# One of four sets of a dense product by seven block products, and a batch of attention one piece later, in a fused attention and MLP kernel

## The chip, the cores and the metric

One Trainium2 chip, one core. The metric is device time in microseconds (us) for one execution, lower is better. Three engines do most of the work: TensorE multiplies matrices, VectorE and ScalarE take its results out of PSUM and work on them (PSUM is the memory that TensorE's products go to, SBUF the one where the program keeps its other tiles). GpSimd does smaller elementwise work, and SyncE issues the transfers. Most executions of one kernel agree within 0.3%; a few lie about 1% higher.

## The reference, cut to what matters

Attention with a decay per head, in blocks of 64 (batch 4, 8 heads, 768 positions, 64 numbers a head), gives x of 3072 x 512. Then comes a dense layer pair with gelu.

```python
for b in range(nb):                      # 12 blocks of 64
    intra = einsum('bhic,bhjc->bhij', qb, kb) * Dmask
    intra = einsum('bhij,bhjd->bhid', intra, vb)
    inter = einsum('bhid,bhde->bhie', qb * lam_pow, kv_state)
    out[:, :, sl] = intra + inter
    kv_state = lam_block * kv_state + einsum('bhsd,bhse->bhde', kb_dec, vb)
...
h = x @ w_in                             # 512 x 2048, the first dense product
return gelu_tanh(h) @ w_out              # 2048 x 512, the second
```

## The kernel before

Attention is cut into 24 steps (4 batches, 3 blocks of 256 positions, 2 halves of the heads). From step 13 on the steps run in pairs (17 alone), called batches here: `burst((18, 19), (16, 17))` computes the scores of 18 and 19, the outputs O of 16 and 17, and the state products K of 18 and 19. The dense work is cut into pieces in a queue, `filler`, and `fill(n)` runs the next n of them between the attention batches, so that TensorE has work while VectorE and ScalarE prepare. Dense work is queued by groups of 256 or 512 tokens; group 4 is the fifth.

```python
groups = [[0, 1], [2], [3], [4, 5], [6, 7], [8, 9], [10, 11]]
SEVEN = (5, 6)                           # groups whose first product uses seven block products
...
def mm1(fs):                             # a plain piece: 4 matmuls of 512 columns, then gelu
    Hps = ps_M.tile([P, per, N], FP32, tag="M", name="Hps")
    for i, f in enumerate(fs):
        for c in range(NC):
            pin(nc.tensor.matmul(by_block(Hps[:, i, :]), w_in16[:, c, f * P : (f + 1) * P], x(c), ...))
    ...
    pin(nc.scalar.activation(out=dst, in_=Hps[:], func=AF.Gelu_apprx_tanh))
...
def sum_x(m):                            # one of four sums of blocks of x, on VectorE, fp16
    pin(nc.vector.tensor_tensor(x_block(m, cs), x_block(a, cs), x_block(b, cs), op))
...
def seven(m, k):                         # product m of set k: 4 matmuls of 256 columns
    ...                                  # into a bank HX (m = 1, 6, 7, 4), HW (2) or HY (5, 3)
    if m == 1:
        copied("m1", "q32", nc.scalar)   # ScalarE copies PSUM into a buffer of the q32 ring
    elif m == 2:
        added(0, 0, "m1")                # VectorE: m1 += HW; its gelu is put on `pending`
    elif m == 5:
        copied("q", "q32", nc.scalar)
        release()                        # runs what is pending
    elif m == 6:
        copied("u2", "k32", nc.vector)
    elif m == 3:
        added(0, 1, "u2")
    elif m == 7:
        added(1, 1, "q")                 # VectorE: q += HX
    elif m == 4:
        pending.insert(0, lambda: gelu(1, 0, dst[:]))
    if k == HF // 2 - 1 and m in (3, 7, 4):
        release()
...
for i in range(HF):                      # groups that use plain pieces
    for fs in ([[i, i + HF]] if per == 2 else [[i], [i + HF]]):
        filler.append(lambda fs=fs: mm1(fs))
```

`prep_qk(n)` is two things: VectorE and ScalarE cast q and k of step n to fp16 (`cast_qk`), and SyncE issues the DMA that transposes them (`transpose_dma`). `prep_v(n)` has GpSimd scale v of step n (`scale_v`) and issues the loads of step n + 3. `causal` is VectorE's masking of the scores. In the part concerned, the order of the program is this:

```python
    cast_qk(16)
    scale_v(16)
    fill(2)
    burst((13, 14), (12,))
    transpose_dma(16)
    ...
    fill(3)
    burst((15, 16), (13, 14))
    ...
    sum_win(4, 1, nc.vector)
    fill(2)
    prep_qk(20)
    fill(1)
    prep_qk(21)
    prep_v(20)
    fill(3)

    burst((18, 19), (16, 17))
    prep_v(21)
    fill(2)
    U(18)
    U(19)
    fill(4)
    prep_qk(22)
    fill(2)
    burst((20, 21), (18, 19), 11, 4)
```

## Time and profile before

| | value |
|---|---|
| time before, three runs | 199.60, 199.63, 201.62 us |
| time of the profiled run | 201.31 us, of which the trace's span is 199.4 us |
| busy | TensorE 96%, VectorE 77%, ScalarE 62%, GpSimd 38% |

The lines themselves stand in the prediction. How to read the table: TensorE is the bound, so only its work and its holes count. The profiled run took 201.31 us (a trace's span is some 1.9 us shorter than the time of its run).

### The profile page before, as it was taken

What the parts mean: (1) busy time and instruction counts of PE and PEld (TensorE: products, weight loads), DVE (VectorE), ACT (ScalarE), POOL (GpSimd) and SP (SyncE); (2) the same over time, 40 slices, a digit from 0 to 9 for tenths busy, and PEclk for the clock granted to TensorE, in tenths of its full rate; (3) what the DMA queues carried; (4) which work ended last, traced back from release to release, by engine and by line L of the source; (5) the groups of instructions that cost most, each with busy time, mean ns of one, the idle gap of its engine ahead of it and who ended that gap; (6) DMA issues with size and microseconds to landing.
All of it is one profiled execution on the core that took longest, in us unless ns stands there. A gap on an engine that the chain in (4) does not pass through costs nothing.

```text
span 199.4 us, 5931 instructions
## 1 busy us (share of the span) xinstructions
PE 191.8 (96%) x2437; PEld 140.4 (70%) x2439; DVE 152.9 (77%) x296; ACT 122.7 (62%) x251; POOL 74.8 (37%) x85
## 2 busy tenths in 40 slices
PE   8979999999999999969999999999999999999993
PEld 2556544456888888634578855578888888888882
DVE  4897623689997889968899927999678997588620
ACT  2673878366793675657764386764668845778321
POOL 6694123457457833547171535347002030002000
PEclk9999999999999999999999999999999999999999
DMA  6999999999999999999993997620202200020205
GB/s 173 290 327 386 386 384 384 294 287 294 327 246 262 219 280 149 221 299 221 302 195 62 249 324 92 184 56 0 52 26 83 104 9 0 0 108 0 105 3 210
DMA packets 61722, 37.86 MB, mean 190 GB/s; under 512 B 17536, under 2 KB 54656, under 8 KB 61696
## 3 DMA queue, kind: packets, MB, share of 16 engines
q1 hardware_dynamic: 61152, 37.23, 73.7%
q8 instruction: 19, 0.31, 0.7%
q10 hardware_dynamic: 544, 0.26, 0.5%
q14 instruction: 7, 0.06, 0.1%
HBM read 27.26 MB, written 6.29 MB: 168 GB/s over the span
## 4 chain that ended last, share of the span: by engine, by line
PE 75%; DMA 15%; SPq 6%; ACT 1%; issue 1%; DVE 1%
PE Hps L542 18%; PE MX L619 17%; PE MY L619 9%; PE HX L711 7%; DMA wi<-in_moe_w_in_dram 7%; DMA k<-in_k_dram 5%; PE MW L619 4%; SPq L70 4%; PE HY L711 4%; PE S L340 3%; PE O2ps L557 3%; DMA qkT<-qk 3%; PE HW L711 2%; SPq L94 2%; PE OK L398 1%; PE O L449 1%
## 5 line engine op out<-in xcount | busy, mean ns | idle before, releaser
L542 PE MATMUL Hps<-xT,w_in 128*128 128x512 f16 (+1 forms) x288 | 50.8, 332 | 0.0
L501 POOL TENSOR_TENSOR u<-t,lumask 128x256 f16<-128x256 f32 x40 | 30.6, 780 | 48.0 <-DVE t L494 30.5
L542 PEld LDWEIGHTS <-w_in 128*128 128x128 f16 x288 | 27.8, 98 | 19.0
L546 ACT ACTIVATE gT<-Hps 128x512 f16<-128x512 f32 x56 | 33.1, 598 | 9.4 <-PE Hps L542 8.8
L350 DVE TENSOR_TENSOR PT<-S,mask 128x512 f16<-128x512 f32 x48 | 30.4, 681 | 7.9 <-PE S L340 7.8
L619 PEld LDWEIGHTS <-gs 128*128 128x128 f16 x320 | 31.2, 98 | 3.6
L266 POOL TENSOR_TENSOR v<-v,dv 128x512 f16<-128x512 f32 x24 | 29.8, 1243 | 8.9 <-DMA v<-in_v_dram 8.4
L619 PEld LDWEIGHTS <-gT 128*128 128x128 f16 x240 | 23.2, 98 | 3.6 <-ACT gT L546 0.5
L619 PE MATMUL MX<-w_sum,gs 128*128 128x256 f16 x160 | 21.4, 273 | 0.0
L664 POOL TENSOR_TENSOR o<-u,q 128x512 f32<-128x512 f32 (+1 forms) x5 | 5.8, 1160 | 37.1 <-ACT u L636 37.1
L278 DVE TENSOR_TENSOR qk<-q,dq 128x512 f16<-128x512 f32 x23 | 19.0, 828 | 0.7 <-DMA q<-in_q_dram 0.6
L283 ACT ACTIVATE qk<-k 128x512 f16<-128x512 f32 x24 | 15.0, 626 | 6.5 <-DMA k<-in_k_dram 6.5
L589 DVE TENSOR_TENSOR gs<-gT 128x1024 f16<-128x1024 f16 (+1 forms) x24 | 16.6, 695 | 2.2 <-ACT gT L546 2.2
L557 PE MATMUL O2ps<-w_out,gT 128*128 128x512 f16 x64 | 14.6, 379 | 0.0
L475 ACT ACTIVATE xT<-OK 128x256 f16<-128x256 f32 x26 | 10.0, 455 | 7.3 <-PE OK L398 7.2
L711 PEld LDWEIGHTS <-ws 128*128 128x128 f16 x128 | 12.5, 98 | 1.8
L636 ACT ACTIVATE u<-MX 128x256 f32<-128x256 f32 x18 | 6.9, 384 | 10.2 <-PE MX L619 10.2
L475 ACT ACTIVATE xT<-O 128x256 f16<-128x256 f32 x22 | 8.0, 459 | 7.5 <-PE O L449 5.0
L340 PEld LDWEIGHTS <-qkT 64*64 64x64 f16 x384 | 6.0, 106 | 8.4 <-issue 2.5
L340 PE MATMUL S<-qkT 64*64 64x128 f16 x384 | 9.2, 221 | 2.6 <-DMA qkT<-qk 1.5
L589 DVE TENSOR_TENSOR gs<-gs,gT 128x1024 f16<-128x1024 f16 (+1 forms) x12 | 10.6, 887 | 0.3
L557 PEld LDWEIGHTS <-gT 128*128 128x128 f16 x64 | 6.1, 98 | 6.6
(95 smaller groups left out, 320.9 us busy)
## 6 DMA issues: line engine op xcount, KB each, us to landing
q<-in_q_dram SPq DMA_DIRECT2D x24, 256.0 KB, 5.1
k<-in_k_dram SPq DMA_DIRECT2D x24, 256.0 KB, 5.1
v<-in_v_dram SPq DMA_DIRECT2D x23, 256.0 KB, 5.3
out_dram<-o SPq DMA_DIRECT2D x19, 256.0 KB, 3.7
wo<-in_moe_w_out_dram SPq DMA_DIRECT2D x4, 1024.0 KB, 9.5
wi<-in_moe_w_in_dram SPq DMA_DIRECT2D x4, 512.0 KB, 8.2
wi<-in_moe_w_in_dram SPq DMA_DIRECT2D x2, 1024.0 KB, 12.8
out_dram<-o SPq DMA_DIRECT2D x2, 512.0 KB, 6.9
```

What stands on the lines that cost most here:

```text
L266: pin(nc.gpsimd.tensor_tensor(wide(tv[:]), ld32[s][2][:], decay(dv, s), ALU.mult))
L278: pin(q_eng.tensor_tensor(wide(tq), q32[:], decay(dq, s), ALU.mult))
L340: pin(nc.tensor.matmul(Sps[hl][half64(c), hp, jk, :], o[half64(hl), 1, jk, hp, half64(c)], o[half64(hl), 0, :, hp, half64(c)], start=True, ...
L350: pin(nc.vector.tensor_tensor(t[:, hl].rearrange("p b c d -> p b (c d)"), Sps[:].rearrange("p b c d -> p b (c d)"), mask[:].unsqueeze(1).t ...
L475: pin(nc.scalar.activation(out=d, in_=o, func=AF.Copy))
L501: pin(nc.gpsimd.tensor_tensor(u[:], state[half][:].unsqueeze(2).to_broadcast([P, 2, 2, D]), lumask[:, 2 * half : 2 * half + 2, :].unsqueez ...
L542: pin(nc.tensor.matmul(by_block(Hps[:, i, :]), w_in16[:, c, f * P : (f + 1) * P], x(c), start=(c == 0), stop=(c == NC - 1)))
L546: pin(nc.scalar.activation(out=dst, in_=Hps[:], func=AF.Gelu_apprx_tanh))
L557: pin(nc.tensor.matmul(O2[tau][0][:], gT[:, f % HF, f // HF, tau * P : (tau + 1) * P], w_out16[:, f, :], start=(n == 0), stop=(n == NF - 1)))
L589: pin(nc.vector.tensor_tensor(g_rows(m, i), g_rows(a, i), g_rows(b, i), op))
L619: pin(nc.tensor.matmul(dst, lhsT, rhs, start=(opens and i == 0), stop=(closes and i == HF - 1), skip_group_check=True))
L711: pin(nc.tensor.matmul(dst[:, i, :], w_in_block(a, slice(c, c + 1), slice(f * P, f * P + P))[:, 0], x_block(b, slice(c, c + 1))[:, 0], sta ...
```

## The change

The intent has two parts. The first: a batch of steps 13 and 14 waited for the transpose of step 14, so it starts one piece later, and the load of v of step 16 moves behind that transpose. The second: one of the four sets of group 4's first product is done by seven products of 256 columns in place of four pieces of 4 x 512, which is an eighth less TensorE work for that set; the preparations of steps 20 and 21 and the batch of 18 and 19 move to fit.

```diff
     SEVEN = (5, 6)
+    MIXED = 4
+    sum_xs = []
...
-            if k == HF // 2 - 1 and m in (3, 7, 4):
+            if (k == HF // 2 - 1 or g == MIXED) and m in (3, 7, 4):
                 release()
...
-        for i in range(HF):
+        if g == MIXED:
+            sum_xs.append(sum_x)
+            plain = [[f] for i in range(2, HF) for f in (i, i + HF)]
+            for m in (1, 0, 2, 5, 0, 6, 3, 0, 7, 4):
+                filler.append((lambda m=m: seven(m, 0)) if m else (lambda fs=plain.pop(0): mm1(fs)))
+            for fs in plain:
+                filler.append(lambda fs=fs: mm1(fs))
+        for i in range(HF) if g != MIXED else ():
...
-        prep_qk(n + 2) if n == 8 else prep(n + 2)
+        prep_qk(n + 2)
+        if n == 11:
+            scale_v(13)
+            load_step(16, "qk")
+        elif n > 8:
+            if n == 12:
+                load_step(16, "v")
+            prep_v(n + 2)
...
-    fill(2)
+    fill(3)
     burst((13, 14), (12,))
...
-    fill(3)
+    fill(2)
     cast_qk(17)
...
-    fill(2)
+    for m in (1, 2, 3, 4):
+        sum_xs[0](m)
     prep_qk(20)
-    fill(1)
+    fill(3)
     prep_qk(21)
+    fill(8)
+
+    burst((18, 19), (16, 17))
     prep_v(20)
-    fill(3)
-
-    burst((18, 19), (16, 17))
-    prep_v(21)
     fill(2)
     U(18)
     U(19)
-    fill(4)
+    prep_v(21)
+    fill(2)
     prep_qk(22)
     fill(2)
     burst((20, 21), (18, 19), 11, 4)
```

(Cut: the numbering of the pieces behind which VectorE's sums for the second product hang, which follows the three pieces more.)

More of the change, by code (lines that the diff above doesn't have):

```diff
@@ L862, in queue_group @@
         else:
-            behind(9, 0, 4, (1, 2) if g == 3 else (1, 2, 4, 3))
+            n1 += 3 * (g == MIXED)
+            behind(n1 - 7, 0, 4, (1, 2) if g == 3 else (1, 2, 4, 3))
             if g == 3:
```

## The prediction

> **What bounds the kernel now.** I read the page first: how busy each engine is, and in which slices.
>
> ```profile
> PE 191.8 (96%) x2437; PEld 140.4 (70%) x2439; DVE 152.9 (77%) x296; ACT 122.7 (62%) x251; POOL 74.8 (37%) x85
> PE   8979999999999999969999999999999999999993
> PEclk9999999999999999999999999999999999999999
> ```
>
> TensorE (PE) is busy for 191.8 of 199.4 us at full clock, so a microsecond counts only if it takes TensorE work away or closes a hole in that row. The row has holes at both ends, which the change does not touch, and one inside: slice 18 of 40 (a slice is 5 us), near 85 to 90 us. Next I asked who waited for whom on TensorE; the longest line is the hole:
>
> ```profile
> PE S L340 <- DMA qkT<-qk: 1.5, 1, 1.5
> ```
>
> The timeline of all engines from 80 to 92 us shows what it is:
>
> ```profile
> 82.39 0.45 SPq L70 DMA_DIRECT2D v<-in_v_dram  x1
> ...
> 83.00 1.72 SPq L293 DMA_TRANSPOSE qkT<-qk  x1
> ...
> 87.05 0.42 PE L340 MATMUL S<-qkT 64*64 64x128 f16 x16
> ...
> 88.41 4.07 SPq L293 DMA_TRANSPOSE qkT<-qk  x2
> ...
> 88.99 0.42 PE L340 MATMUL S<-qkT 64*64 64x128 f16 x16 [1.52 <-DMA qkT<-qk]
> ...
> 89.96 2.32 PE L542 MATMUL Hps<-xT,w_in 128*128 128x512 f16 x10
> ```
>
> This is the batch of steps 13 and 14. Scores of 13 run at 87.05; scores of 14 wait 1.52 us for the transposed q and k of step 14, whose transpose entered the queue at 83.00 behind the loads of q, k and v of step 16. The two transposes at 88.41 are those of 15 and 16, which matter below. The chain of waits gives that transpose's landing:
>
> ```profile
> 83.00 5.94 DMA qkT<-qk
> ```
>
> So it landed at 88.94. From there to the end the chain is TensorE nearly throughout.
>
> **What the Trainium skill says.** "TensorE: Matmul & The Clock Gate", Back-to-back issue gap, gives 262 cycles for 256 columns and 518 for 512, that is 109 and 216 ns at 2.4 GHz. The trace agrees: 28 matmuls of 512 columns fill 6.04 us of the chain (216 ns each), and four of 256 take a slot of 0.44 us. "DMA: Bandwidth & Descriptors", Queues, rings and completion order, says that each DMA engine takes descriptors in ring order. The trace agrees in direction: the transpose behind three loads took 5.94 us, one issued at 107.10 with no DMA running took 3.2. "VectorE: DVE Perf Modes", perf-mode tier table, has tensor_tensor at single rate with a PSUM operand and at double rate with 16-bit SBUF operands; here 0.69 us for an add of 512 columns from PSUM, 0.41 us for an fp16 sum of 512 columns. It agrees.
>
> **The change, part by part.** (1) The batch of 13 and 14 starts one dense piece later (4 matmuls of 512, 0.87 us), and the load of v16 moves behind the transpose of 14. Scores of 13 then begin at 87.05 + 0.87 = 87.92, those of 14 want to begin at 88.2. The transpose is issued 0.6 us earlier (82.4) with one 256 KB load less ahead (estimate 0.9 us at about 290 GB/s), so it should land near 88.05. The wait of **1.52 us goes**, entirely or all but 0.1.
>
> (2) The next batch (15 and 16) then comes sooner, but its transposes do not. The issuing queue is serial: the transpose of 15 is at 88.41 after the same set of issues, that of 16 at about 90.3 behind it. Those near there took 5.0 to 5.2 us to land, so 16 lands near 95.3. TensorE gets there earlier than before: scores of 14 at 88.2, dense work from 89.17, six pieces (24 x 0.216 = 5.2) instead of seven, scores of 15 at 94.45, of 16 at 94.73. A **new wait of about 0.6 us** on the transpose of 16 (in the kernel before TensorE came at 96.4, after the landing).
>
> (3) One of four sets of group 4's first product: 4 pieces of 4 x 512 columns (16 x 0.218 = 3.49 us) become 7 products of 4 x 256 (7 x 0.438 = 3.07 us). **0.42 us less TensorE work.** VectorE gets four fp16 sums (some 1.5 us), three adds and a copy (4 x 0.69); ScalarE two copies more (0.60 each). Before, VectorE stood idle 3.60 us ahead of the causal masks of that batch and ScalarE also had gaps, and the batch itself moves some 1.3 us back, so as totals they fit.
>
> (4) But the products share one PSUM bank HX, and they are queued as 1, 2, 5, 6, 3, 7, 4 with plain pieces after 1, 5 and 3 and **none between 7 and 4**. The built program's list of waits confirms it: the first matmul of 4 waits for VectorE's add that reads HX after 7. Group 5 already does the same products, spaced. Its timeline gives the latency:
>
> ```profile
> 140.06 0.60 PE L711 MATMUL HX<-xs,ws 128*128 128x256 f16 x4
> 140.49 0.60 PE L619 MATMUL MX<-w_sum,gs 128*128 128x256 f16 x4
> 140.69 0.69 DVE L732 TENSOR_TENSOR q<-HX,q 128x512 f32<-128x512 f32 x1
> ```
>
> Product 7 starts at 140.06, VectorE's add runs from 140.69 to 141.38. TensorE's next piece started at 140.49, so an adjacent product 4 would have stood for 141.38 - 140.49 = 0.89 us plus a few hundredths for the signal: **0.93 us added**. The other waits inside the set (6 on ScalarE's copy of 1, 3 on its copy of 5, 7 on VectorE's copy of 6) have 0.15 to 0.4 us to spare by my placing of the pieces.
>
> (5) The batch of 18 and 19 now stands after more pieces, and between it and the batch of 20 and 21 six pieces are left instead of eight: 5.25 us instead of 7.0. What has to happen inside that gap is not shorter. The transposes of 20 and 21 reuse buffers that the batch of 18 and 19 still reads; in the kernel before they were issued back to back:
>
> ```profile
> 113.86 1.69 SPq L643 DMA_DIRECT2D out_dram<-o  x2
> 120.57 2.65 SPq L293 DMA_TRANSPOSE qkT<-qk  x2
> ```
>
> The new order of the queue puts the second 512 KB output store between the two (it moved behind the transpose of 20, which blocks it until the batch is done). With X the issue of transpose 20, 1.75 us after the batch's start, transpose 21 was issued at X + 1.4 and landed at X + 5.5; now it is issued at about X + 2.2 with 512 KB ahead of it (estimate 1.4 us of data), landing between X + 6 and X + 7. Scores of 21 used to be due at about X + 7.3, now at X + 5.5. Likewise GpSimd's scaling of v20 and v21 moved into the gap: before, GpSimd did two u, v21 and two u in 4.3 us; one more scaling of 1.2 us ends about 8.7 us after the batch's start, where the K product of 21 is due at about 8.2. The two waits lie on top of each other, so the longer counts: **0.7 us added**, from 0.4 to 1.7.
>
> Sum: -1.52 + 0.6 - 0.42 + 0.93 + 0.7 = **+0.3 us**, so 199.63 + 0.29 = 199.9 us. After the batch of 20 and 21 the two programs have the same work left and TensorE is the bound to the end, so a shift there reaches the end whole.
>
> **The rivals.** First, the plain one that the intent suggests: the hole closes, the set saves its columns, no new wait: 199.63 - 1.52 - 0.42 = 197.7 us. Against it speaks the wait of 4 on 7, which the build shows, and the fixed issue of transpose 16. For it, that the order of the preparations was moved with some care. Second, transposes 16 and 21 land in time (the lag from data to landing varies) and only the wait of 4 on 7 stays: -1.52 - 0.42 + 0.93 = -1.0, so 198.6 us. Third, transpose 21 lands last behind the store, at X + 7.2 or later, and the small waits inside the set bite as well: +1 us more than my sum, 200.9 us. Fourth, VectorE becomes the bound around 105 to 120 us, where it has no idle time before the 3.60 us: then the waits spread over the set and come to some 0.5 us more, inside the third.
>
> **Range and chances.** The ends are the second and the third: 198.6 to 200.9. A step of 2% is 4 us; the largest gain I can construct is 1.9 us and the largest loss some 2, so "within 2%" has nearly all the chance: 0.02 faster, 0.97 same, 0.01 slower. The sign is close to open, leaning a little to slower.
>
> **What would show it.** In the changed profile: the 1.5 us wait of the scores on a transpose near 88 us is gone; a wait of 0.3 to 0.9 us on a transpose stands at the scores of step 16 near 95 us; a TensorE hole of about 0.9 us ahead of the last HX product near 119 us, released by VectorE's q add; a wait for a transpose or for GpSimd's v at the batch near 127 to 129 us. The prediction is wrong if the hole ahead of the last product is missing, if transpose 16 moves earlier together with TensorE, or if transpose 21 lands before its scores are due: each makes it faster by 0.6 to 0.9 us.

## The result, and the profile after

The changed kernel took 202.32 us as the median of six runs (201.91 to 203.12); the kernel before beside it took 199.62 (199.53 to 201.62, six runs). Ratios here are the mean time of one kernel's fast runs over that of the other's of the same rounds, so they are not quite the ratio of these medians: 1.012, 95% interval 1.0078 to 1.0163. That is within the 2% that counts as the same, but slower, and above the range that the prediction gave.

The page of the changed kernel: TensorE is as busy as before, but the span is 201.3 us.

```profile
PE 192.3 (96%) x2451; PEld 141.5 (70%) x2451; DVE 159.8 (79%) x304; ACT 123.8 (61%) x253; POOL 74.7 (37%) x85
PE   8979999999999999998999989799999999999993
```

The hole of slice 18 is gone, and there are new ones in slices 19, 24 and 26: one between 90 and 96 us, two between 115 and 131 us. Busy time doesn't show the 0.42 us that the set saves; the profile only models the ends of matmuls, so I count from starts below. TensorE's waits in the changed kernel (total, times, longest):

```profile
PE S L340 <- DMA qkT<-qk: 1.9, 2, 1.1
...
PE HX L713 <- DVE q L734: 0.8, 1, 0.8
...
PE Hps L544 <- DVE PT L350: 0.5, 1, 0.5
```

The first of the experiments ran the kernel before again, unchanged. That profile is of a run of 199.67 us, its span is 197.8 us, and it is the one to compare with. TensorE's longest wait in it is one at the start of the kernel, and no wait for a transpose is left:

```profile
...
PE idle L181 <- PEq L1083: 0.8, 1, 0.8
```

TensorE's timeline of this usual run of the kernel before, from the batch of 13 and 14 to the first dense piece after the batch of 20 and 21 (start, duration, what; x32 is the scores of two steps in one row, x16 of one):

```profile
87.08 0.64 PE L340 MATMUL S<-qkT 64*64 64x128 f16 x32
...
103.99 0.42 PE L340 MATMUL S<-qkT 64*64 64x128 f16 x16
...
117.19 0.64 PE L340 MATMUL S<-qkT 64*64 64x128 f16 x32
...
125.92 0.64 PE L340 MATMUL S<-qkT 64*64 64x128 f16 x32
...
127.46 2.75 PE L542 MATMUL Hps<-xT,w_in 128*128 128x512 f16 x12
```

The same places in the changed kernel, with the wait ahead of a row in brackets:

```profile
87.89 0.64 PE L340 MATMUL S<-qkT 64*64 64x128 f16 x32
...
95.67 0.42 PE L340 MATMUL S<-qkT 64*64 64x128 f16 x16 [0.84 <-DMA qkT<-qk]
...
104.98 0.42 PE L340 MATMUL S<-qkT 64*64 64x128 f16 x16
...
118.54 0.60 PE L713 MATMUL HX<-xs,ws 128*128 128x256 f16 x4
119.92 0.60 PE L713 MATMUL HX<-xs,w_in 128*128 128x256 f16 x4 [0.78 <-DVE q L734]
120.45 0.64 PE L340 MATMUL S<-qkT 64*64 64x128 f16 x32
...
127.45 0.42 PE L340 MATMUL S<-qkT 64*64 64x128 f16 x16
...
128.93 0.42 PE L340 MATMUL S<-qkT 64*64 64x128 f16 x16 [1.06 <-DMA qkT<-qk]
...
131.00 2.75 PE L544 MATMUL Hps<-xT,w_in 128*128 128x512 f16 x12 [0.50 <-DVE PT L350]
```

From that last row to the end both take 70.3 us, so the whole difference is ahead of it. From the scores of step 17 (103.99 before, 104.98 after) to that row it is 23.47 us before and 26.02 after: 2.55 us more. In parts:

- To the scores of 18 it is 2.27 us more. Two plain pieces, 1.75 us, moved ahead of that batch, and the set saves 0.42; that makes 1.33 of it. The other **0.94 us** is the hole ahead of product 4. The starts say the same: product 4 starts 1.38 us behind product 7, where undisturbed products start 0.44 us apart.
- From there to the scores of 20 it is 1.73 us less, which is the two pieces that moved away.
- From there to the dense row it is 3.55 us instead of 1.54: **2.01 us** more. The scores of 21 start 1.48 us behind those of 20, in the rerun of the kernel before 0.25, so 1.23 is the transpose of 21. The other 0.78 is VectorE: the dense row waits for its masks.

### The profile page after: what moved, and what is told of

Read it like the earlier page. It is cut to its first block, busy times and chain, and to the rows that moved or that the text cites. A ratio compares the mean times of both kernels' runs of the same rounds, so it can differ in the third digit from the quotient of the medians.

```text
span 201.3 us, 5970 instructions
## 1 busy us (share of the span) xinstructions
PE 192.3 (96%) x2451; PEld 141.5 (70%) x2451; DVE 159.8 (79%) x304; ACT 123.8 (61%) x253; POOL 74.7 (37%) x85
## 4 chain that ended last, share of the span: by engine, by line
PE 81%; DMA 6%; DVE 5%; SPq 4%; issue 1%; ACT 1%
PE Hps L544 18%; PE MX L621 17%; PE MY L621 9%; PE HX L713 8%; PE O2ps L559 7%; PE MW L621 4%; PE HY L713 4%; SPq L70 4%; DMA wi<-in_moe_w_in_dram 4%; PE Hps L804 3%; PE S L340 3%; DMA qkT<-qk 3%; PE HW L713 2%; DVE gs L591 2%; DVE PT L350 2%; PE OK L398 2%
## 5 line engine op out<-in xcount | busy, mean ns | idle before, releaser
L544 PE MATMUL Hps<-xT,w_in 128*128 128x512 f16 (+1 forms) x272 | 47.7, 329 | 0.5 <-DVE PT L350 0.5
L544 PEld LDWEIGHTS <-w_in 128*128 128x128 f16 x272 | 26.2, 98 | 17.4 <-issue 0.6
L548 ACT ACTIVATE gT<-Hps 128x512 f16<-128x512 f32 x52 | 30.7, 602 | 8.7 <-PE Hps L544 8.2
L621 PEld LDWEIGHTS <-gT 128*128 128x128 f16 x240 | 23.2, 98 | 3.6 <-ACT gT L548 0.5
L591 DVE TENSOR_TENSOR gs<-gT 128x1024 f16<-128x1024 f16 (+1 forms) x24 | 19.1, 802 | 1.2 <-ACT gT L548 1.2
L278 DVE TENSOR_TENSOR qk<-q,dq 128x512 f16<-128x512 f32 x23 | 19.6, 853 | 0.6 <-DMA q<-in_q_dram 0.5
L713 PEld LDWEIGHTS <-ws 128*128 128x128 f16 x144 | 14.0, 97 | 2.4
L713 PEld LDWEIGHTS <-w_in 128*128 128x128 f16 x108 | 10.5, 98 | 2.6 <-issue 1.0
L713 PE MATMUL HX<-xs,ws 128*128 128x256 f16 x72 | 10.8, 273 | 0.0
```

What stands on the lines that cost most here:

```text
L278: pin(q_eng.tensor_tensor(wide(tq), q32[:], decay(dq, s), ALU.mult))
L591: pin(nc.vector.tensor_tensor(g_rows(m, i), g_rows(a, i), g_rows(b, i), op))
L621: pin(nc.tensor.matmul(dst, lhsT, rhs, start=(opens and i == 0), stop=(closes and i == HF - 1), skip_group_check=True))
L713: pin(nc.tensor.matmul(dst[:, i, :], w_in_block(a, slice(c, c + 1), slice(f * P, f * P + P))[:, 0], x_block(b, slice(c, c + 1))[:, 0], sta ...
```

## The experiments

Two theories went into the first round. V: the 1.52 us hole near 88 us belongs to the one profiled run of the kernel before and not to its usual run, so part 1 of the change gains nothing. L: part 1 does gain, and the set loses still more than the timeline says. Each kernel is given as an edit of the kernel before or of the changed one. Medians of different rounds are compared only by their distance from the kernel before of the same round, which was 199.6 to 199.9 us throughout.

**b_again**: the kernel before, no edit.

> The kernel before, unchanged, to get a second profile of it. Its first profile has a span of 199.4 us and comes from a run of 201.3 us, while its timed runs are mostly 199.6 us: the profile may show a run that is not the usual one. Theory H (the hole is usual): the span is 199.4 again or near it, and the wait of the scores of step 14 on its transpose is 1 us or more. Theory V (the hole varies): the span is about 197.8 us and the wait near 88 us is 0.3 us or less, so that closing it was worth nothing in the usual run and the whole of the loss is the four new waits. Time: ratio 1.000 within 0.005.

Measured: 199.99 us (199.59 to 200.72), ratio 1.0016 [0.9995, 1.0036]; the hole near 88 us isn't there (the timeline above). SyncE's queue shows why. The first two rows are from the first profile of the kernel before, the transposes of steps 12 and 13:

```profile
71.46 4.13 SPq L293 DMA_TRANSPOSE qkT<-qk  x1
...
78.09 3.01 SPq L293 DMA_TRANSPOSE qkT<-qk  x1
```

The same two in the rerun:

```profile
71.36 1.80 SPq L293 DMA_TRANSPOSE qkT<-qk  x1
...
75.65 1.70 SPq L293 DMA_TRANSPOSE qkT<-qk  x1
```

In the first profile these two issues took 4.13 and 3.01 us, in the rerun 1.80 and 1.70, and the queue reached the transpose of 14 at 83.00 instead of 81.27. Why an issue sometimes takes 4 us I can't say. That the other long runs of the kernel before (5 of 68 in all were above 201 us) have the same hole isn't shown either: no second one of them was profiled. The profiles of `set_only` and `b_qk22` below, which leave this part as it was, don't have it.

**a_only**: part 1 alone, on the kernel before.

```diff
-        prep_qk(n + 2) if n == 8 else prep(n + 2)
+        prep_qk(n + 2)
+        if n == 11:
+            scale_v(13)
+            load_step(16, "qk")
+        elif n > 8:
+            if n == 12:
+                load_step(16, "v")
+            prep_v(n + 2)
...
-    fill(2)
+    fill(3)
     burst((13, 14), (12,))
...
-    fill(3)
+    fill(2)
```

> The kernel before with only the first part of the change: the batch of 13 and 14 one piece later, the load of v16 behind the transpose of 14. Theory H: gains 1.5 us at the scores of 14, loses 0.7 to 0.9 at the scores of 16 (transpose of 16 lands near 95.4), so 0.6 us faster, 199.0 us. Theory V: no gain to be had; the time is equal within 0.3 us or up to 0.8 us slower if the wait for the transpose of 16 is new.

Measured: 199.84 us, ratio 1.0008 [0.999, 1.0026]. Part 1 is worth nothing in usual runs.

**set_only**: the changed kernel with part 1 undone.

```diff
-        prep_qk(n + 2)
-        if n == 11:
...
-            prep_v(n + 2)
+        prep_qk(n + 2) if n == 8 else prep(n + 2)
...
-    fill(3)
+    fill(2)
     burst((13, 14), (12,))
...
-    fill(2)
+    fill(3)
```

> The changed kernel with the first part undone: the set of seven products and the moved preparations stay, the batch of 13 and 14 and the load of v16 are as in the kernel before. By the two traces, from the start of the set on, the change loses 0.94 (product 4 behind 7), 1.2 (scores of 21) and 0.6 (VectorE's masks) and saves 0.42 of TensorE work: 2.3 us slower than the kernel before, 201.9 us. If the losses were due to the first part (TensorE arriving earlier at transposes that do not), it is less than 1.5 us slower.

Measured: 202.58 us (201.91 to 204.23), ratio 1.0161 [1.0124, 1.0199]. From the scores of 17 to the dense row it takes 26.01 us, like the changed kernel's 26.02, with the same three waits. So the whole loss is the set and the preparations that moved with it, and theory V stands.

**spaced**: one plain piece between products 7 and 4, taken from the gap ahead of the batch of 20 and 21.

```diff
-            for m in (1, 0, 2, 5, 0, 6, 3, 0, 7, 4):
+            for m in (1, 0, 2, 5, 0, 6, 3, 0, 7, 0, 4):
...
-    fill(8)
+    fill(9)
     burst((18, 19), (16, 17))
...
-    fill(2)
+    fill(1)
     U(18)
```

> The changed kernel with one plain piece between products 7 and 4 of the set (and so one piece fewer after the batch of 18 and 19). Theory: VectorE's add of 0.69 us hides behind a piece of 0.87 us, TensorE's hole of 0.78 us ahead of product 4 is gone, but the gap between the batches has 5 pieces instead of 6, so the wait at the scores of 21 is up to 0.87 us longer: time within 0.3 us of the changed kernel. Rival: the wait at the scores of 21 is bound to the issue of its transpose, which follows the batch of 18 and 19 wherever that stands, so removing the hole just moves it: the sum of the two waits stays at 1.8 to 2.1 us.

Measured: 202.11 us, ratio 1.0148 [1.0108, 1.0189], like the changed kernel. (Its profile fell on an unusually long run, so only its waits are used.) The hole ahead of 4 is gone, and the scores of 21 wait that much longer:

```profile
129.27 0.42 PE L340 MATMUL S<-qkT 64*64 64x128 f16 x16 [2.00 <-DMA qkT<-qk]
```

(That is 0.94 us more than the 1.06 of the changed kernel.)

The second round asked about the gap ahead of the batch of 20 and 21. SyncE's queue in the changed kernel has the transposes of 20 and 21 with an output store between them, as predicted:

```profile
122.20 2.00 SPq L293 DMA_TRANSPOSE qkT<-qk  x1
124.31 0.52 SPq L645 DMA_DIRECT2D out_dram<-o  x1
125.00 1.53 SPq L293 DMA_TRANSPOSE qkT<-qk  x1
```

VectorE's timeline in the changed kernel ends the gap with the cast of step 22's q and the masks of 20 and 21:

```profile
125.44 1.42 DVE L591 TENSOR_TENSOR gs<-gs,gT 128x1024 f16<-128x1024 f16 x1
...
128.81 1.53 DVE L278 TENSOR_TENSOR qk<-q,dq 128x512 f16<-128x512 f32 x1
130.26 2.47 DVE L350 TENSOR_TENSOR PT<-S,mask 128x512 f16<-128x512 f32 x4
```

The same in the rerun of the kernel before:

```profile
123.19 0.98 DVE L589 TENSOR_TENSOR gs<-gs,gT 128x1024 f16<-128x1024 f16 x1
...
125.72 0.68 DVE L278 TENSOR_TENSOR qk<-q,dq 128x512 f16<-128x512 f32 x1
126.39 2.48 DVE L350 TENSOR_TENSOR PT<-S,mask 128x512 f16<-128x512 f32 x4
```

**store_first**: the transpose of 20 one piece later, so that the store precedes it and the two transposes are issued together.

```diff
+    fill(1)
     prep_qk(20)
-    fill(3)
+    fill(2)
     prep_qk(21)
```

> The changed kernel with one thing mended: the second output store of the group before is issued ahead of the transpose of 20 again, not between the transposes of 20 and 21. Theory D (VectorE's queue is what limits the gap between the two batches): the wait of the scores of 21 on their transpose (1.06 us in the changed kernel) shrinks by 0.5 us or more, but the masks of 20 still begin when VectorE has done its work (130.3 us), so the wait for them grows by about as much and the time stays within 0.3 us of the changed kernel's 202.3. Theory T (the transpose limits): the time falls by the length of the wait, to 201.3 us or less.

Measured: 203.14 us, ratio 1.0146 [1.0101, 1.019]. The scores of 21 no longer wait, and nothing is won: the next wait was ready right behind the first. TensorE in this run:

```profile
129.67 0.32 PE L438 MATMUL K<-v,qk 64*64 64x64 f16 x16 [0.98 <-POOL v L266]
...
130.82 2.75 PE L544 MATMUL Hps<-xT,w_in 128*128 128x512 f16 x12 [0.50 <-DVE PT L350]
```

GpSimd's scaling of v21 and VectorE's masks end about when the transpose used to. The prediction had the first of these ("the two waits lie on top of each other"); the masks it had not.

**qk22_late**: step 22's casts and transpose behind the batch of 20 and 21.

```diff
-    prep_qk(22)
     fill(2)
     burst((20, 21), (18, 19), 11, 4)
+    prep_qk(22)
```

> The changed kernel with the preparation of q and k of step 22 (1.5 us on VectorE in that place) moved behind the batch of 20 and 21, so that VectorE reaches the masks of 20 sooner. The transposes stay as they are. Theory D: the wait of TensorE on the masks (0.50 us at 131.0) is gone, the wait of the scores of 21 (1.06 us) stays: 0.5 to 0.7 us faster than the changed kernel, 201.7 us. Theory T: the masks are late only because the scores are: no change.

Measured: 201.65 us, ratio 1.0085 [1.0038, 1.0132]. The wait for the masks is gone and the one for the transpose of 21 stays at 1.09 us. Against the kernel before of its round it loses 1.9 us by the medians, where the changed kernel lost 2.7 of its own. In the profiles, scores of 17 to dense row take 25.35 us instead of 26.02, 0.67 less: most of the masks' 0.78 us, so their share of the gap was real and had its own cause.

**b_qk22**: the control, the same edit on the kernel before.

> A control: the kernel before with q and k of step 22 prepared behind the batch of 20 and 21, as in the mended kernel. VectorE's masks kept TensorE nowhere in the kernel before, so the ratio should be 1.000 within 0.002; if it is faster, part of what the mended kernel gains is not the set's.

Measured: 199.93 us, ratio 1.0008 [0.9988, 1.0029]. The kernel before, whose cast took 0.68 us, has nothing to win there.

**gap9**: three pieces more ahead of the batch of 20 and 21.

```diff
     prep_qk(22)
-    fill(2)
+    fill(5)
     burst((20, 21), (18, 19), 11, 4)
```

> The changed kernel with nine plain pieces between the batches of 18, 19 and of 20, 21 instead of six (7.9 us for 5.2), the last three taken from behind. Both waits in the gap, on the transpose of 21 and on the masks, should be gone (1.06 and 0.50 us by the records, 1.9 us of start times), and only the hole ahead of product 4 stays: 0.5 us slower than the kernel before, 200.4 us. If the time stays above 201.5 us, what is lost in that stretch is not the shortness of the gap.

Measured: 208.13 us, ratio 1.0398 [1.0352, 1.0444]; a clear miss. The waits in the gap are gone (20 and 21 in one row at 130.81). But the batch also sets where the sevenfold sets of group 5 fall against the attention that follows, and there VectorE now comes late (also 1.38 us for the masks at 163.31):

```profile
143.15 0.60 PE L713 MATMUL HX<-xs,ws 128*128 128x256 f16 x4 [2.26 <-DVE u L726]
```

The recorded waits, with the 0.78 us ahead of product 4, come to 5.6 of the 8.4 us by which this profile is longer than that of `b_again`. That the place of the sets is the reason is read from these waits; no run tested it.

**repaired**: the order of `spaced`, the store first, and two pieces more in the gap.

```diff
-            for m in (1, 0, 2, 5, 0, 6, 3, 0, 7, 4):
+            for m in (1, 0, 2, 5, 0, 6, 3, 0, 7, 0, 4):
...
+    fill(1)
     prep_qk(20)
-    fill(3)
+    fill(2)
     prep_qk(21)
-    fill(8)
+    fill(9)
...
     prep_qk(22)
-    fill(2)
+    fill(4)
     burst((20, 21), (18, 19), 11, 4)
```

> The changed kernel with three things mended together: a plain piece between products 7 and 4, eight plain pieces in the gap between the batches, and the store ahead of the transposes. No TensorE wait of the change is left, and the 0.42 us of saved columns should show: 0.2 to 0.5 us faster than the kernel before, ratio 0.998. Rival: the set costs more than it saves even when spaced (more weight loads, VectorE and ScalarE fuller), and the ratio is 1.003 or more.

Measured: 205.44 us, ratio 1.0265 [1.0226, 1.0304]; a miss of the same kind as `gap9` (waits of 1.73 us for VectorE's u and 1.03 us for its masks in group 5's stretch).

The third round mended without moving the batches.

**order7**: the same seven products and the same three plain pieces, with the piece that stood behind product 1 moved between 7 and 4.

```diff
-            for m in (1, 0, 2, 5, 0, 6, 3, 0, 7, 4):
+            for m in (1, 2, 5, 0, 6, 3, 0, 7, 0, 4):
```

> The changed kernel with the same three plain pieces placed otherwise in the set: 1, 2, 5, piece, 6, 3, piece, 7, piece, 4, so that each product that waits for a copy or an add out of its bank has at least 0.87 us of other work ahead, and the gap between the batches keeps six pieces. If the 0.78 us hole ahead of product 4 was a cost of its own, the batch of 18 and 19 comes 0.9 us earlier and all that follows with it, the waits in the gap staying what they are: 0.8 to 1.0 us faster than the changed kernel, 201.4 us. If the waits in the gap are tied to something that does not move with the batch, they grow by as much and the time stays at 202.3.

Measured: 201.37 us (201.1 to 201.75), ratio 1.0082 [1.006, 1.0104]; 1.77 us above the kernel before, where the changed kernel is 2.70 above. The hole ahead of product 4 is its own cost, of about the size predicted: by the medians its removal gained 0.93 us, and in the profiles the way from the scores of 17 to the dense row is 25.29 us instead of 26.02, 0.73 less (the K products now wait 0.27 us for ScalarE's gelu).

**gap_mended**: the three edits for the gap together: store first, step 22 late, and v20 scaled ahead of the batch.

```diff
+    fill(1)
     prep_qk(20)
-    fill(3)
+    fill(2)
     prep_qk(21)
+    scale_v(20)
     fill(8)

     burst((18, 19), (16, 17))
-    prep_v(20)
+    load_ahead(23)
+    prep_v(21)
     fill(2)
     U(18)
     U(19)
-    prep_v(21)
     fill(2)
-    prep_qk(22)
     fill(2)
     burst((20, 21), (18, 19), 11, 4)
+    prep_qk(22)
```

> The changed kernel with all three limits of the gap taken away and the numbers of pieces kept: the store ahead of the transposes of 20 and 21, v20 scaled on GpSimd before the batch of 18 and 19, q and k of 22 prepared behind the batch of 20 and 21. Waits of TensorE at the scores of 21, at the K products and on the masks should be gone or under 0.3 us together; the hole ahead of product 4 stays. 0.5 us slower than the kernel before (0.94 less 0.42): 200.2 us. If one of the limits was not the cause, that wait shows again in the profile and the time is over 201 us.

Measured: 201.3 us (201.18 to 201.38), ratio 1.0075 [1.0055, 1.0096]; better than the change, and 1 us short of what I expected. The transposes and v are in time; 0.78 us ahead of product 4 (not mended here) and 0.40 us for the masks remain, and a 0.38 us wait for VectorE's gs further on is new.

**mended**: `gap_mended` with the order of `order7`.

> Both mendings together: the order of the set as in the run with the other placing, and the gap mended. Only the saved columns stay: 0.42 us less than the kernel before, 199.3 us, ratio 0.998. If the set costs something that the records of waits do not show, the ratio is 1.000 or more.

Measured: 201.27 us, ratio 1.0085 [1.0058, 1.0112]; a miss by 2 us. Two mends that were each worth about 1 us are together worth no more than one. A wait inside the set stands where the hole was:

```profile
116.21 0.60 PE L713 MATMUL HY<-xT,ws 128*128 128x256 f16 x4 [0.81 <-ACT q L724]
```

ScalarE's copy of product 5 goes into a buffer of the ring that holds the loaded q; this one still held step 20's, which VectorE's cast frees, and the cast stood behind the four sums.

**cast_early**: `mended` with that cast ahead of the sums, and its transpose where it was.

```diff
     sum_win(4, 0, nc.vector)
+    cast_qk(20)
     fill(2)
...
     fill(1)
-    prep_qk(20)
+    transpose_dma(20)
     fill(2)
```

> The doubly mended kernel with q and k of step 20 cast before the four sums of the set, so that the buffer for ScalarE's copy of product 5 is free in time. If that buffer was the cause, the wait of product 3 on ScalarE (0.81 us) is gone and the kernel is 0.8 us faster than the doubly mended one: 200.5 us, ratio 1.004. If the wait only came from ScalarE being full, it stays and the time is 201.3 us.

Measured: 201.18 us, ratio 1.0086 [1.0046, 1.0125]. The wait is gone, so the buffer was its cause, but the time is 0.7 us above what I expected: product 7 now waits 0.44 us for VectorE's copy of product 6. The same work is late one step further on.

**mended3**: `cast_early`, with the gelu of product 4 ahead of that of 7, and step 22 fifteen pieces after the batch instead of right behind it.

```diff
-            if (k == HF // 2 - 1 or g == MIXED) and m in (3, 7, 4):
+            if k == HF // 2 - 1 and m in (3, 7, 4) or g == MIXED and m in (3, 4):
                 release()
...
     burst((20, 21), (18, 19), 11, 4)
-    prep_qk(22)
...
-    fill(20)
+    fill(12)
+    prep_qk(22)
+    fill(8)
```

> As the run before, and ScalarE's activation of product 4 goes ahead of that of product 7 (its bank is waited for by the K products of step 19: 0.27 us), and q and k of step 22 are prepared 12 pieces later, behind the sums that the MY products waited for (0.37 us). If the set costs nothing but waits, none is left and the saved 0.42 us show: ratio 0.998 to 1.000, 199.3 us. If new waits appear in the next group's sets, or the ratio stays at 1.003 or more, the work that the set adds to VectorE and ScalarE is more than this stretch of the kernel can hide.

Measured: 201.72 us, ratio 1.0115 [1.008, 1.015]. No gain; two waits for VectorE's copy (0.44 and 0.71 us) and one of 0.30 for the masks. (Its profile, too, is of one of its longer runs.)

By now a new theory was due: VectorE's time as such is the cost, and where the wait shows depends only on the order.

**nosum**: `cast_early` without the four sums of x; the products read plain blocks of x. This one is wrong (relative error 0.307); TensorE's work is the same.

```diff
         def x_block(t, cs):
+            if t in X_SUMS and g == MIXED:
+                t = X_SUMS[t][0] if t in (1, 4) else X_SUMS[t][2]
+                t = t if isinstance(t, tuple) else (1, 1)
...
-    for m in (1, 2, 3, 4):
-        sum_xs[0](m)
```

> The kernel with the early cast, without the four sums of the set: wrong result on purpose. If VectorE's time is what the set costs, the wait of product 7 on the copy of 6 (0.44 us) is gone and the sums of the MY products come earlier too: 0.4 to 0.8 us faster than with the sums (201.2 us), about 200.6 us. If TensorE's products cost more than the columns they save, nothing changes.

Measured: 200.54 us, ratio 1.0033 [1.0014, 1.0052], 0.95 us above the kernel before of its round, where `cast_early` was 1.48 above: the sums cost about half a microsecond of the end (the two intervals still touch, so the size is rough; this profile is of the longest of the seven runs). Busy times in the stretch that holds the set, 104 to 120 us (window, its length, then busy us of TensorE, its weight loads, VectorE, ScalarE and GpSimd, the granted clock, DMA share and GB/s). The rerun of the kernel before:

```profile
104.00:120.00 16.00, 16.00 (x246) 11.93 (x246) 12.40 (x19) 8.97 (x21) 5.61 (x4) 1.00 0.76 198
```

The changed kernel:

```profile
104.00:120.00 16.00, 15.22 (x163) 12.16 (x161) 14.88 (x24) 8.99 (x19) 3.76 (x3) 1.00 0.78 187
```

`cast_early`, from which `nosum` differs by the sums alone:

```profile
104.00:120.00 16.00, 15.56 (x184) 12.04 (x185) 14.90 (x23) 8.84 (x19) 5.25 (x4) 1.00 0.81 205
```

Without the sums:

```profile
104.00:120.00 16.00, 16.00 (x194) 12.79 (x196) 12.58 (x20) 9.09 (x20) 5.01 (x4) 1.00 0.89 215
```

VectorE has 14.88 of 16 us of work in the changed kernel, and TensorE loses 0.78. In `cast_early` it has 14.90, and TensorE loses 0.44; without the sums it has 12.58, and TensorE is full in this stretch. (In the kernel before, the window already holds the masks of 18 and 19.)

**nosum_k**: `nosum` with the gelu order of `mended3`; wrong as well.

> The same, with ScalarE's activation of product 4 ahead of that of product 7 as well (the 0.27 us wait of the K products): 0.3 us faster than the run before, 200.3 us; only if all waits were gone would the saved 0.42 us show, 199.3 us.

Measured: 200.58 us, ratio 1.0051 [1.0022, 1.0079]; no faster than `nosum`, where I expected 0.3 us. (One of its six runs, of 204.13 us, counts as slow and is left out of the ratio.) From the scores of 17 to those of 20 it takes 21.62 us, against 21.93 in the kernel before: here at last the set's saving is seen, 0.31 of the 0.42 us. It is given back: from the scores of 20 to the dense row this profile takes 2.09 us instead of 1.54, and from there to the end 0.75 us more than that of `b_again`. The waits on record in these two parts are 0.23 us for the masks of 20 and 21 and 0.37 us for VectorE's gs; the rest has no wait on record.

No version was faster than the kernel before.

## Why the prediction was wrong

The direction was right (+0.3 us predicted, slower), the size wrong: +2.7 us by the medians, beyond the end of the range at +1.3. Step 1 of the sum failed, and step 5 was far too small. By its own steps:

1. **The hole near 88 us, −1.52: this step failed.** The mechanism was read rightly, but it belonged to one run. The profiled run took 201.31 us, the median was 199.63, and 199.63 already contains no such hole. I subtracted from the median a wait that only a profile of a slower run had. `b_again` and `a_only` show 0 in place of −1.52. (The landing at 88.05 takes off the 0.9 us of the load but not also the 0.6 us of the earlier issue; nothing hangs on it.)
2. **The new wait for the transpose of 16, +0.6: right in kind, small in size.** It is 0.84 us in the changed kernel's own profiled run, the longest of its six, and 0 to 0.45 in the profiles of the versions that keep part 1. With step 1 it was to give −0.92; in the usual runs it gives about 0.
3. **The saved columns, −0.42: right.** The sections around the set add up with it, and `nosum_k` shows 0.31 us of it in the open.
4. **The hole ahead of product 4, +0.93: right.** It measured 0.94, and taking it away gained 0.73 by the profile and 0.93 by the medians (`order7`).
5. **The gap between the batches, +0.7: right in kind, mis-sized.** It measured 2.01, above its own 0.4 to 1.7. The transpose alone is 1.23: it was issued at X + 2.8 and not X + 2.2, since the issue of 20 ahead of it took 2.00 us, and landed at X + 6.7, inside the stretch that I gave. The other 0.78 is VectorE, which this step left out: I reckoned the gap for SyncE and GpSimd alone.

With what was measured the sum is 0 + 0 - 0.42 + 0.94 + 2.01 = +2.5 us, near the +2.7 of the medians.

The fourth rival, VectorE as the bound, came true in part, but I had looked for it in the wrong place and gave it 0.5 us. I set the totals of VectorE against idle time ahead of the masks and concluded that "as totals they fit". They do: the set adds seven adds and sums and a copy to VectorE, and of the 3.60 us of idle time ahead of the masks of 18 the changed kernel still has 1.04 there and 0.82 inside the set. But with less idle time, an instruction that comes late is likelier to show at its reader; that is argued and not tested by itself. In `mended` and `cast_early` mending one wait brought up another that led back to VectorE's order; in `spaced` and `store_first` the next ones were for the transpose and for GpSimd's v, ahead of the masks, and VectorE doesn't explain those two. `nosum` shows what the sums alone do: taking them away, with TensorE's work left alone, removed the waits inside the set and about 0.5 of 1.5 us. The other 0.95 us has no experiment: the three adds and the copy stayed in all of these versions.

In the gap there is a second part. Between the starts of the two sets of masks VectorE ran the same instructions in both kernels; this took 8.73 us before, 1.04 of them idle, and 9.35 after, none idle, so 1.66 us more for the same work. The rows above show part of it: 0.98 became 1.42, and 0.68 became 1.53. GpSimd's timeline in the changed kernel shows what ran beside them:

```profile
124.81 1.49 POOL L266 TENSOR_TENSOR v<-v,dv 128x512 f16<-128x512 f32 x1
...
128.31 1.49 POOL L266 TENSOR_TENSOR v<-v,dv 128x512 f16<-128x512 f32 x1
```

The slow add at 125.44 and the slow cast at 128.81 each lie beside a scaling of v, two of which now fall into the gap. The Trainium skill, "SBUF — State Buffer", Who interferes with whom, says that a VectorE instruction with two SBUF inputs contends with a GpSimd instruction that reads SBUF, over a lock that one of them holds; one with at most one SBUF input, outside the two-port modes, does not. The traces agree. In the profiles of `b_again` and the changed kernel together, the 13 casts of q with no GpSimd instruction beside them took 0.68 us each, and the 11 with a scaling of v beside them for more than 0.5 us took 1.0 to 1.75. A mask, which reads one input from PSUM, took 0.67 to 0.69 us in both cases (57 with no GpSimd instruction beside them, 30 with one for more than 0.3 us). The masks of 20 and 21 above, 2.47 and 2.48 us for four, say nothing of it, since GpSimd stood idle beside them. No run moved the scaling alone; the share that it has in the 0.78 us is read from the timeline.

What stays open: what the 0.95 us that `nosum` leaves are, whether some order lets the set pay, and why the issue of a transpose is at times so slow.

## What to carry to other kernels

Before reading a hole from a profile, set the time of the profiled run against the median of the runs: a profile of a run that is 1% longer may show a hole that the median doesn't have. Work that is taken off the bound engine and put on one that it fills to 93% in that stretch can cost more than it saves: here idle time of the second engine, with the order as it was, kept its results punctual. Count it by stretch, and count beside which other engine's work it falls. When a wait is mended and another of the same size takes its place, stop moving instructions and take the suspected engine's work away once, even with a wrong result, to see what it costs.

## What the Trainium skill lacked or had wrong

- "Perfetto Trace Analysis", Optimization Strategy, says to find the gaps on the engine that bounds and what they wait for. It doesn't say to check first that the traced run is a usual one: here the trace of a 201.31 us run had a gap of 1.52 us, and that of a 199.67 us run of the same kernel had none.
- "DMA: Bandwidth & Descriptors", DMA Transpose (X-bar), gives no spread for the issue of a transpose. The same 256 KB transpose took from 1.23 to 4.13 us to issue within one run of the kernel before, and 3.1 to 7.6 us from issue to landing.
- "SBUF — State Buffer", Who interferes with whom, has the rule, but for a size only two measurements (6.8 and 1.5 times) without the instructions that they belong to. Beside GpSimd's scaling of v the cast of q took 1.53 us instead of 0.68 (1.0 to 1.75 us in 11 casts).
